# One-tensor scalar steps, and a denominator product on VectorE in place of a sum on GpSimd, in a delta-rule and rational-MoE kernel

## The chip, the cores and the metric

The kernel runs on one core of one Trainium2 chip. The metric is device time in microseconds. A core has five engines that run their own instruction queues strictly in order and meet through semaphores: TensorE (in the profile PE, its weight loads PEld), VectorE (DVE), ScalarE (ACT), GpSimd (POOL) and SyncE (SP, which here only issues DMAs). SBUF is the memory that all engines work in; PSUM takes the matrix products and is read here by DVE and ACT. Every number comes from one profiled execution or from the three timed runs.

## What is computed

The inputs are q, k and v of shape (4, 8, 768, 48), beta of (4, 8, 768), and the weights, in float64, of an MLP with a rational activation. First a delta rule runs over time for each of the 32 heads, with a 48 x 48 state:

```python
k_n = k / (norm(k) + 1e-6)
for t in range(S):
    y[t]  = q[t] @ state
    state = state + beta[t] * outer(k_n[t], v[t] - k_n[t] @ state)
```

Its output, as x with 3072 rows (tokens) of 384, goes through the MLP of width 2048:

```python
h = x @ w_in
P = a[0] + a[1]*h + a[2]*h**2 + a[3]*h**3
Q = 1.0 + abs(b[0])*abs(h) + abs(b[1])*h**2
out = (P / (Q + 1e-6)) @ w_out
```

## The kernel before, in words

Time is cut into 12 chunks of 64 steps. A chunk's delta rule is solved with products of blocks on PE and a small triangular inversion on DVE (`inverse`). Its 256 tokens then pass the MLP in 8 units of 256 hidden columns each, so there are 96 units. Float32 values are split in two float16 parts and multiplied in three passes.

A unit n goes through four functions. `hidden` lets PE build h in PSUM (`ph`, two buffers, 128 partitions x 512 values). `numerator` lets ACT make u = A3*h + a2 (tile `mu`, line L843), z = B0*|h| (tile `mr`, L845) and w = (R1*h)^2 (tile `mw`, L847); POOL adds z to w (L848); DVE makes u = h*u (L849) and u = (u + A1)*h (L850). `quotient` lets ACT compute r = exp(-ln(w + Q0)) (L861, L862, in the buffer of z); DVE multiplies g = (u + A0)*r into the float16 tile `mg` (L867), makes w = (w + Q0)*g (L868) and u = u + A0 - w (L872), and POOL writes u*r as g's second part (L873). In four of the eight units of the middle chunks, POOL takes over A0 (L854) and the subtraction (L870), and DVE's product is L865. `accumulate` multiplies g by w_out on PE. Each of `mu`, `mr`, `mw` and `mg` has three buffers. The factors A3 to Q0 are columns of tile `msc`, one value per partition.

Around each chunk there are small steps on one value, or 16, per partition. `keys_normalized` computes the keys' inverse norms in tile `nrm` (128 x 16, L513 to L520). `scales` has tile `sc`, `tokens` tile `sf`, and `scale_of` makes a power of two by masking the bits of a float against the tile `tmask` (L263). `scalars` evaluates a bound on the activation from the tile `horner` and the token scales in tile `kp` (L786 to L806) and multiplies the table `tab` by six columns of `sf` into `msc` (L810). It runs once per chunk, twice for the first: 13 times. Most of these steps are products or sums of two tensors in SBUF on DVE.

The weights arrive at the start as float64 words; `to_f32` turns them into float32 in 56 pieces: ACT takes the absolute value, POOL the maximum with a smallest number (L333), DVE joins the bits (L334, L341).

The order on each engine is set by a scheduler that goes through the functions in the order written at the end of the kernel (a unit's numerator, the quotient of the unit before, a share of the attention of later chunks, the accumulation of the unit before that, the next unit's hidden part), with priorities for some attention steps and a model of durations. The diff therefore also moves instructions that it does not name.

Of the kernel before, what the change touches and what calls it, by code (L numbers as in the profile page):

```python
# [34 lines left out]
def kernel(
# [125 lines left out]
    horner = cpool.tile([P, 2, 4], F32, name="horner")  # L161
    nc.vector.memset(horner[:, 1], 0.0)
    nc.vector.memset(horner[:, 1, 2:3], 1.0)
    for i, (at, frm) in enumerate((((0, 0), 9), ((0, 1), 11), ((0, 2), 10), ((0, 3), 7), ((1, 0), 8), ((1, 1), 10))):
        nc.vector.tensor_copy(horner[:, at[0], at[1] : at[1] + 1], coef[:, frm : frm + 1])
# [89 lines left out]

    def scale_of(dst, ss, nm, root=0):


# [2 lines left out]
        nc.scalar.activation(lg, ss, AF.Ln)
        nc.scalar.activation(lg, lg, AF.Exp, scale=-0.5 / (1 + root), bias=consts[:, 1 + root : 2 + root])
        nc.vector.tensor_tensor(  # L263
            out=dst.bitcast(U32), in0=lg.bitcast(U32), in1=tmask[:, :n], op=ALU.bitwise_and
        )
        return lg
# [13 lines left out]
    rb = cpool.tile([P, 3], F32, name="rb")  # L280
    rb0, rb1, sb1 = (rb[:, i : i + 1] for i in range(3))
    nc.vector.tensor_scalar_max(sb1, b1, 2.0 ** -90)
    nc.scalar.activation(rb0, sb1, AF.Ln)
    nc.scalar.activation(rb0, rb0, AF.Exp, scale=0.5)
    nc.vector.tensor_mul(rb1, rb0, rb0)
    nc.vector.tensor_sub(sb1, sb1, rb1)
    nc.vector.reciprocal(rb1, rb0)
    nc.vector.tensor_scalar(sb1, sb1, rb1, 0.5, op0=ALU.mult, op1=ALU.mult)
    nc.vector.tensor_add(sb1, sb1, rb0)
# [35 lines left out]
    def to_f32(t, src, nm, keep=MIN_NORMAL):  # L325
# [7 lines left out]
        nc.gpsimd.tensor_scalar_max(a, a, keep)  # L333
# [171 lines left out]
    def keys_normalized(c):  # L505
# [7 lines left out]
        nc.vector.tensor_scalar_max(ss, ss, 2.0 ** -94)  # L513
# [29 lines left out]
    def inverse(c):  # L543
# [10 lines left out]
        nc.vector.tensor_copy(wt[:, 0:256:17], bblk[:, c])  # L554
# [220 lines left out]
    def scalars(c, lo, hi):  # L775
# [11 lines left out]
        nc.vector.tensor_mul(hm, wn, gm)

        nc.vector.tensor_mul(t, horner[:, 0], hm.broadcast_to([P, 4]))
        nc.vector.tensor_add(t, t, horner[:, 1])  # L790
# [275 lines left out]
```

## Time and profile before

| | |
|---|---|
| median of three timed runs | 918.05 us (916.96 to 919.3) |
| the profiled execution | 918.86 us |
| its span, first to last instruction | 917.1 us |
| busy DVE / PE / POOL / ACT | 842.7 / 678.4 / 604.4 / 576.3 us |
| mean granted TensorE clock | 0.931 |
| first unit's w on ACT starts | 153.8 us |

A row of an engine's groups reads: line, engine, operation, output tile <- input tiles, shapes, count | busy time in us, mean duration of one in ns | idle time of the engine just before these instructions, and what ended it. A row of the timeline reads: start, duration, engine, line, operation, tiles. A row of the waits reads: engine, tile and line that waited, what it waited for, us in total, times, longest. In a row of stretches, the stretch's length is followed by busy time and number of instructions of PE, PEld, DVE, ACT and POOL as far as they have any, then the granted clock, the DMA engines' busy share and GB/s. A row of one tile's instructions has minimum, median and maximum duration in ns, and the first and the last start.

### The profile page before, as it was taken

How to read it: one execution, taken by the hardware profiler on the slowest of the kernel's cores; microseconds unless marked ns; L12 is line 12 of the kernel's file. 1: busy time of each engine (PE TensorE's matmuls, PEld its weight loads, DVE VectorE, ACT ScalarE, POOL GpSimd, SP SyncE). 2: the span in 40 equal slices, each digit the busy share in tenths (PEclk: the TensorE clock that was granted, in tenths of full speed). 3: DMA queues.
4: the chain of work that ended last, by engine and by line, in shares of the span. 5: the costliest groups of instructions: out<-in, count | busy, mean ns of one | idle time of the engine just before them, and what ended most of it. 6: DMA issues, size and time to landing. Idle time of an engine off the chain costs nothing.

```text
span 917.1 us, 23581 instructions
## 1 busy us (share of the span) xinstructions
PE 678.4 (74%) x9264; PEld 542.9 (59%) x9264; DVE 842.7 (92%) x1657; ACT 576.3 (63%) x1099; POOL 604.4 (66%) x479
## 2 busy tenths in 40 slices
PE   0321453877787886986798988888989798999785
PEld 0221443665575775765676876766767676766563
DVE  5999998887997999899999999999999999898976
ACT  4765776556466575666565766657657566677473
POOL 6866965636456376767677677676767665666754
PEclk9999996887989998999998989989989999999998
DMA  7969888679897779779268578468476662200000
GB/s 228 222 162 188 192 180 155 94 132 155 149 130 154 137 136 149 131 147 179 42 132 152 98 157 141 81 151 146 67 185 98 122 114 36 64 2 19 1 18 18
DMA packets 420110, 111.49 MB, mean 122 GB/s; under 512 B 361376, under 2 KB 416672, under 8 KB 420000
## 3 DMA queue, kind: packets, MB, share of 16 engines
q1 hardware_dynamic: 417824, 108.83, 63.5%
q8 instruction: 72, 1.18, 0.6%
q10 hardware_dynamic: 2176, 1.17, 0.4%
q14 instruction: 38, 0.31, 0.1%
HBM read 40.47 MB, written 26.23 MB: 73 GB/s over the span
## 4 chain that ended last, share of the span: by engine, by line
DVE 44%; issue 13%; DMA 11%; ACT 9%; PE 8%; POOL 8%; SPq 6%; POOLq 0%; DVEq 0%; ACTq 0%
DVE mw L868 5%; DVE mu L849 3%; DVE mg L867 3%; DVE mg L865 3%; DVE mu L850 3%; DVE z L238 3%; SPq L449 3%; PE po L888 2%; POOL mw L848 2%; DVE mu L872 2%; PE ph L826 2%; DMA wsi<-in_moe_w_in_dram 2%; DVE pr L586 2%; DMA tq<-xdq 2%; PE pg L417 1%
## 5 line engine op out<-in xcount | busy, mean ns | idle before, releaser
L888 PE MATMUL po<-w_out,mg 128*128 128x384 f16 x1152 | 225.9, 341 | 23.7 <-POOL mg L873 12.6
L826 PE MATMUL ph<-xT,w_in 128*128 128x256 f16 x1728 | 226.7, 284 | 19.7 <-DVE mu L850 19.3
L826 PEld LDWEIGHTS <-w_in 128*128 128x128 f16 x1728 | 173.2, 102 | 58.4 <-DVE mu L850 18.3
L873 POOL TENSOR_TENSOR mg<-mu,mr 128x512 f16<-128x512 f32 x96 | 131.2, 1367 | 76.5 <-DVE mu L872 34.6
L848 POOL TENSOR_TENSOR mw<-mw,mr 128x512 f32<-128x512 f32 x96 | 135.6, 1413 | 65.2 <-ACT mw L847 63.7
L888 PEld LDWEIGHTS <-mg 128*128 128x128 f16 x1152 | 112.3, 102 | 96.0 <-POOL mg L873 17.4
L417 PEld LDWEIGHTS <-kbd 128*128 128x128 f16 x1680 | 93.6, 119 | 45.4 <-issue 41.2
L843 ACT ACTIVATE mu<-ph,coef,msc 128x512 f32<-128x512 f32 x96 | 74.3, 774 | 44.8 <-DVE msc L810 15.4
L861 ACT ACTIVATE mr<-mw,msc 128x512 f32<-128x512 f32 x96 | 69.5, 726 | 50.2 <-POOL mw L848 49.8
L868 DVE SCALAR_TENSOR_TENSOR mw<-mw,msc,mg 128x512 f32<-128x512 f32 x96 | 96.3, 1003 | 1.2
L849 DVE TENSOR_TENSOR mu<-ph,mu 128x512 f32<-128x512 f32 x96 | 65.3, 681 | 16.8 <-ACT mw L847 14.2
L417 PE MATMUL pu<-z,ebd 128*128 128x48 f16 x1728 | 57.9, 188 | 25.8 <-DVE z L238 21.8
L417 PEld LDWEIGHTS <-ebd 128*128 128x128 f16 x1728 | 55.6, 100 | 30.9 <-issue 25.1
L870 POOL TENSOR_TENSOR mu<-mu,mw 128x512 f32<-128x512 f32 x36 | 48.0, 1332 | 38.1 <-DVE mw L868 26.3
L850 DVE SCALAR_TENSOR_TENSOR mu<-mu,msc,ph 128x512 f32<-128x512 f32 x96 | 71.4, 744 | 0.8
L867 DVE SCALAR_TENSOR_TENSOR mg<-mu,msc,mr 128x512 f16<-128x512 f32 x60 | 65.9, 1098 | 2.9 <-ACT mr L862 2.7
L847 ACT ACTIVATE mw<-ph,msc 128x512 f32<-128x512 f32 x96 | 66.5, 692 | 0.0
L845 ACT ACTIVATE mr<-ph,msc 128x512 f32<-128x512 f32 x96 | 65.6, 683 | 0.0
L872 DVE SCALAR_TENSOR_TENSOR mu<-mu,msc,mw 128x512 f32<-128x512 f32 x60 | 64.0, 1067 | 0.4
L417 PEld LDWEIGHTS <-wbd 128*128 128x128 f16 x1152 | 38.1, 103 | 43.0 <-issue 37.8
L862 ACT ACTIVATE mr<-mr 128x512 f32<-128x512 f32 x96 | 60.7, 633 | 1.5
L234 ACT ACTIVATE z<-pu,zmask 128x384 f16<-128x384 f32 x72 | 40.1, 579 | 32.4 <-PE pu L417 22.9
(216 smaller groups left out, 1491.4 us busy)
## 6 DMA issues: line engine op xcount, KB each, us to landing
wsi<-in_moe_w_in_dram SPq DMA_DIRECT2D x24, 256.0 KB, 5.3
xdk<-kn SPq DMA_DIRECT2D x12, 512.0 KB, 3.4
kbd<-tk SPq DMA_DIRECT2D x24, 256.0 KB, 5.1
gd<-g SPq DMA_DIRECT2D x24, 256.0 KB, 4.3
xdq<-kn SPq DMA_DIRECT2D x12, 512.0 KB, 4.5
wso<-in_moe_w_out_dram SPq DMA_DIRECT2D x32, 192.0 KB, 4.0
mbd<-mm SPq DMA_DIRECT2D x24, 256.0 KB, 4.9
wc<-img SPq DMA_DIRECT2D x24, 256.0 KB, 5.5
```

Source lines behind the costliest of these rows:

```text
L417: nc.tensor.matmul(dst[p][:, h], head(bd, lp, p * H + h), head(rt, rp, p * H + h), start=start and n == 0 and h == 0, stop=stop and n == l ...
L826: nc.tensor.matmul(ph[:, i], w_in[:, f2, wp, cc, i * P : (i + 1) * P], x[:, xp, cc], start=k == 0, stop=k == 3 * NCC - 1,)
L843: nc.scalar.activation(u, ph, AF.Identity, scale=A3, bias=a2)
L848: nc.gpsimd.tensor_add(w, w, z)
L849: nc.vector.tensor_mul(u, ph, u)
L850: nc.vector.scalar_tensor_tensor(out=u, in0=u, scalar=A1, in1=ph, op0=ALU.add, op1=ALU.mult)
L861: nc.scalar.activation(r, w, AF.Ln, bias=Q0)
L867: nc.vector.scalar_tensor_tensor(out=g[:, 0], in0=u, scalar=A0, in1=r, op0=ALU.add, op1=ALU.mult)
L868: nc.vector.scalar_tensor_tensor(out=w, in0=w, scalar=Q0, in1=g[:, 0], op0=ALU.add, op1=ALU.mult)
L872: nc.vector.scalar_tensor_tensor(out=u, in0=u, scalar=A0, in1=w, op0=ALU.add, op1=ALU.subtract)
L873: nc.gpsimd.tensor_mul(g[:, 1], u, r)
L888: nc.tensor.matmul(po[p], g[:, gp, i, p * P : (p + 1) * P], w_out[:, f2, wp, i], start=f2 == lo and i == 0 and k == 0, stop=f2 == hi - 1 a ...
```

## The change

In the unit, z becomes B1*|h| (`tab` row 1 now holds b1 times the squared output scale), the Square on ACT and the sum on POOL go, DVE computes w = (z + B0)*h with h read from PSUM, and ACT takes |w|. Since B0 and B1 are not negative, |(B1*|h| + B0)*h| is B1*h^2 + B0*|h|, as before.

The small steps on DVE that took two SBUF tensors now take one tensor and one or two pointer scalars (a value per partition, read as an operand of its own) or constants. `horner`, `tmask` and the square root of b1 (`rb`) are gone. Four of the keys' steps move from DVE to POOL, the copy of beta into `wt` and a copy into `sf` are done by ACT. On POOL the one-operation maxima become a minimum with 3e38 and a maximum.

```diff
+POWER = 0xFF800000
...
+    def power_of_two(dst, src):
+        nc.vector.tensor_scalar(dst.bitcast(U32), src.bitcast(U32), POWER, None, op0=ALU.bitwise_and)
+    def times(dst, x, by, then=None):
+        if then is None:
+            nc.vector.tensor_scalar(dst, x, by, None, op0=ALU.mult)
+        else:
+            nc.vector.tensor_scalar(dst, x, by, then, op0=ALU.mult, op1=ALU.mult)
...
     def scale_of(dst, ss, nm, root=0):
-        nc.vector.tensor_tensor(
-            out=dst.bitcast(U32), in0=lg.bitcast(U32), in1=tmask[:, :n], op=ALU.bitwise_and
-        )
+        power_of_two(dst, lg)
...
     def tables(lo, hi):
-        nc.vector.tensor_scalar_mul(row[1], ro, sb1)
+        nc.vector.tensor_scalar_mul(row[1], io, b1)
...
     def to_f32(t, src, nm, keep=MIN_NORMAL):
-        nc.gpsimd.tensor_scalar_max(a, a, keep)
+        nc.gpsimd.tensor_scalar(a, a, 3.0e38, keep, op0=ALU.min, op1=ALU.max)
...
     def keys_normalized(c):
-        nc.vector.tensor_scalar_max(ss, ss, 2.0 ** -94)
+        nc.gpsimd.tensor_scalar(ss, ss, 3.0e38, 2.0 ** -94, op0=ALU.min, op1=ALU.max)
...
-        nc.vector.tensor_mul(y1, y1, ss)
-        nc.vector.tensor_add(y0, y0, y1)
-        nc.vector.tensor_scalar(y0, y0, 1.0 / 32.0, 1e-6 / 16.0, op0=ALU.mult, op1=ALU.add)
+        nc.gpsimd.tensor_mul(y1, y1, ss)
+        nc.gpsimd.tensor_add(y0, y0, y1)
+        nc.gpsimd.tensor_scalar(y0, y0, 1.0 / 32.0, 1e-6 / 16.0, op0=ALU.mult, op1=ALU.add)
...
     def inverse(c):
-        nc.vector.tensor_copy(wt[:, 0:256:17], bblk[:, c])
+        nc.scalar.copy(wt[:, 0:256:17], bblk[:, c])
...
     def scalars(c, lo, hi):
         nc.vector.reciprocal(gm, d["lg"])
-        nc.vector.tensor_mul(hm, wn, gm)
-        nc.vector.tensor_mul(t, horner[:, 0], hm.broadcast_to([P, 4]))
-        nc.vector.tensor_add(t, t, horner[:, 1])
-        nc.vector.tensor_mul(t[:, 0:2], t[:, 0:2], hm.broadcast_to([P, 2]))
-        nc.vector.tensor_scalar_add(t[:, 1:2], t[:, 1:2], 1.0)
-        nc.vector.reciprocal(t[:, 1:3], t[:, 1:3])
-        nc.vector.tensor_mul(t[:, 0:1], t[:, 0:1], hm)
-        nc.vector.tensor_mul(r, t[:, 0:4:3], t[:, 1:3])
-        nc.vector.tensor_add(gm, r[:, 0:1], r[:, 1:2])
-        nc.vector.tensor_add(gm, gm, m0)
-        nc.vector.tensor_mul(gm, gm, io)
+        times(hm, wn, gm)
+        affine(top_, hm, m3, m2)
+        times(top_, top_, hm, hm)
+        affine(low, hm, b1, b0)
+        affine(low, low, hm, 1.0)
+        affine(one, hm, b0, 1.0)
+        nc.vector.reciprocal(kp[:, 5:7], kp[:, 5:7])
+        times(lin, hm, m1, one)
+        affine(gm, top_, low, lin)
+        nc.vector.tensor_scalar(gm, gm, m0, io, op0=ALU.add, op1=ALU.mult)
...
-        nc.vector.tensor_tensor(out=rk.bitcast(U32), in0=rk.bitcast(U32), in1=tmask[:, :1], op=ALU.bitwise_and)
-        nc.vector.reciprocal(sf[:, 1:2], rk)
-        nc.vector.tensor_mul(ikap, sf[:, 1:2], sf[:, 1:2])
-        nc.vector.tensor_mul(sf[:, 3:4], sf[:, 2:3], ikap)
-        nc.vector.tensor_mul(sf[:, 4:6], sf[:, 2:4], sf[:, 2:3].broadcast_to([P, 2]))
+        power_of_two(rk, rk)
+        nc.vector.reciprocal(rk, rk)
+        times(ikap, rk, rk)
+        nc.scalar.copy(sf[:, 1:2], ikap)
+        times(sf[:, 3:4], sf[:, 2:3], ikap)
+        times(sf[:, 4:6], sf[:, 2:4], sf[:, 2:3])
...
     def numerator(n):
-        nc.scalar.activation(z, ph, AF.Abs, scale=B0)
+        nc.scalar.activation(z, ph, AF.Abs, scale=B1)
+        nc.vector.tensor_mul(u, ph, u)
         w = sb.tile([P, 2, TG], F32, tag="mw", name=f"mw{n}", bufs=MB)
-        nc.scalar.activation(w, ph, AF.Square, scale=R1)
-        nc.gpsimd.tensor_add(w, w, z)
-        nc.vector.tensor_mul(u, ph, u)
+        nc.vector.scalar_tensor_tensor(out=w, in0=z, scalar=B0, in1=ph, op0=ALU.add, op1=ALU.mult)
+        nc.scalar.activation(w, w, AF.Abs)
```

`affine(dst, x, by, plus)` is one tensor_scalar on DVE, x*by + plus. In `scales`, the running maximum of v and the product of two scales take the same form.

Two places show what the scheduler makes of it. The first is DVE's queue at units 45 and 46, where the small steps of chunk 6 (`sf_6`, `kp_6`) lie between the units' products and the solver's (`z_7`). Before:

```order
L263 TENSOR_TENSOR sf_6_8849<-lgx6_8857,tmask_99 128x1
L786 RECIPROCAL kp_6_0_8922<-lgx6_8857 128x1
L865 TENSOR_TENSOR mg45_8993<-mu45_8905,mr45_8907 128x512
L767 RECIPROCAL sf_6_8849<-sf_6_8849 128x1
L787 TENSOR_TENSOR kp_6_0_8922<-top_149,kp_6_0_8922 128x1
L238 SCALAR_TENSOR_TENSOR xT_6_8847<-px_6_0_8862,sf_6_8849,xT_6_8847 128x3x128
L868 SCALAR_TENSOR_TENSOR mw45_8909<-mw45_8909,msc_5_7793,mg45_8993 128x512
L789 TENSOR_TENSOR kp_6_0_8922<-horner_105,kp_6_0_8922 128x4
```

After:

```order
L838 TENSOR_TENSOR mu46_8961<-ph_46_8942,mu46_8961 128x512
L840 SCALAR_TENSOR_TENSOR mw46_8966<-mr46_8963,msc_5_7773,ph_46_8942 128x512
L757 RECIPROCAL sf_6_8829<-sf_6_8829 128x1
L257 TENSOR_SCALAR kp_6_0_8902<-top_138,kp_6_0_8902 128x1
L233 SCALAR_TENSOR_TENSOR xT_6_8827<-px_6_0_8842,sf_6_8829,xT_6_8827 128x3x128
L233 SCALAR_TENSOR_TENSOR xT_6_8827<-px_6_1_8848,sf_6_8829,xT_6_8827 128x3x128
L842 SCALAR_TENSOR_TENSOR mu46_8961<-mu46_8961,msc_5_7773,ph_46_8942 128x512
L857 TENSOR_TENSOR mg45_8973<-mu45_8885,mr45_8887 128x512
```

The small steps are now TENSOR_SCALAR, the new product (L840) stands right behind the product of u, and the products of unit 46 from PSUM have moved ahead of the quotient of unit 45.

The second place is ACT's queue at units 48 to 50. Before:

```order
L861 ACTIVATE mr48_9249<-mw48_9251,msc_6_8943 128x512
L862 ACTIVATE mr48_9249<-mr48_9249 128x512
L861 ACTIVATE mr49_9377<-mw49_9379,msc_6_8943 128x512
L843 ACTIVATE mu50_9634<-ph_50_9615,coef_101,msc_6_8943 128x512
L845 ACTIVATE mr50_9636<-ph_50_9615,msc_6_8943 128x512
L847 ACTIVATE mw50_9638<-ph_50_9615,msc_6_8943 128x512
L862 ACTIVATE mr49_9377<-mr49_9377 128x512
```

After, where L841 is the new Abs, L853 and L854 are the old L861 and L862, and `y_7` and `xT_7` are the attention's outputs on their way to the MLP:

```order
L841 ACTIVATE mw48_9232<-mw48_9232 128x512
L853 ACTIVATE mr48_9229<-mw48_9232,msc_6_8923 128x512
L734 ACTIVATE y_7_9785<-py_7_0_9687,sc_7_7006 128x384
L734 ACTIVATE y_7_9785<-py_7_1_9688,sc_7_7006 128x384
L854 ACTIVATE mr48_9229<-mr48_9229 128x512
L241 ACTIVATE xT_7_9977,xs_7_9978<-y_7_9785 128x768
L841 ACTIVATE mw49_9360<-mw49_9360 128x512
L835 ACTIVATE mu50_9614<-ph_50_9595,coef_99,msc_6_8923 128x512
L837 ACTIVATE mr50_9616<-ph_50_9595,msc_6_8923 128x512
L853 ACTIVATE mr49_9357<-mw49_9360,msc_6_8923 128x512
```

The Abs of unit 49 now stands behind the outputs of the attention and ahead of the first two steps of unit 50.

More of the change, by code (lines that the diff above doesn't have):

```diff
@@ L153 @@
     nc.gpsimd.memset(consts[:, 2:3], 5.5 * LN2)
-    tmask = cpool.tile([P, 4], U32, name="tmask")
-    nc.gpsimd.memset(tmask, 0xFF800000)
     coef = cpool.tile([P, 12], F32, name="coef")
@@ L160 @@
     nc.scalar.activation(coef[:, 6:12], coef[:, 0:6], AF.Abs)
[L161 to L165, printed above, removed]
     a0, a1, a2, a3 = (coef[:, i : i + 1] for i in range(4))
-    m0, _, _, _, b0, b1 = (coef[:, i : i + 1] for i in range(6, 12))
+    m0, m1, m2, m3, b0, b1 = (coef[:, i : i + 1] for i in range(6, 12))
     bblk = cpool.tile([P, NCH, 16], F32, name="bblk")
@@ L278 @@
     top = cpool.tile([P, 3, 2], F32, name="top")
[L280 to L289, printed above, removed]
     def tables(lo, hi):
@@ L639, in scales @@
         if "v" in fmax:
-            nc.vector.tensor_max(sc[:, 1:2], sc[:, 1:2], fmax["v"])
+            nc.vector.tensor_scalar(sc[:, 1:2], sc[:, 1:2], fmax["v"], None, op0=ALU.max)
         fmax["v"] = sc[:, 1:2]
@@ L643, in scales @@
         nc.vector.tensor_copy(sc[:, 4:5], sc[:, 3:4])
-        nc.vector.scalar_tensor_tensor(
-            out=sc[:, 5:6], in0=sc[:, 2:3], scalar=1.0 / 16.0, in1=sc[:, 3:4], op0=ALU.mult, op1=ALU.mult
-        )
+        times(sc[:, 5:6], sc[:, 2:3], 1.0 / 16.0, sc[:, 3:4])
         nc.vector.reciprocal(sc[:, 4:6], sc[:, 4:6])
@@ L782, in scalars, with affine @@
         kp = sb.tile([P, 10], F32, tag="kp", name=f"kp_{c}_{lo}", bufs=4)
-        gm, rk, ikap, hm = (kp[:, i : i + 1] for i in range(4))
-        t = kp[:, 4:8]
-        r = kp[:, 8:10]
+        gm, rk, ikap, hm, top_, low, one, lin = (kp[:, i : i + 1] for i in range(8))
         nc.vector.reciprocal(gm, d["lg"])
-        nc.vector.tensor_mul(hm, wn, gm)
-        nc.vector.tensor_mul(t, horner[:, 0], hm.broadcast_to([P, 4]))
-        nc.vector.tensor_add(t, t, horner[:, 1])
-        nc.vector.tensor_mul(t[:, 0:2], t[:, 0:2], hm.broadcast_to([P, 2]))
-        nc.vector.tensor_scalar_add(t[:, 1:2], t[:, 1:2], 1.0)
-        nc.vector.reciprocal(t[:, 1:3], t[:, 1:3])
-        nc.vector.tensor_mul(t[:, 0:1], t[:, 0:1], hm)
-        nc.vector.tensor_mul(r, t[:, 0:4:3], t[:, 1:3])
-        nc.vector.tensor_add(gm, r[:, 0:1], r[:, 1:2])
-        nc.vector.tensor_add(gm, gm, m0)
-        nc.vector.tensor_mul(gm, gm, io)
+        times(hm, wn, gm)
+        def affine(dst, x, by, plus):
+            nc.vector.tensor_scalar(dst, x, by, plus, op0=ALU.mult, op1=ALU.add)
+        affine(top_, hm, m3, m2)
[7 more added lines that the diff above has]
+        nc.vector.tensor_scalar(gm, gm, m0, io, op0=ALU.add, op1=ALU.mult)
         nc.vector.tensor_scalar_max(gm, gm, 2.0 ** -60)
@@ L839, in numerator @@
         d = unit[n]
-        A3, R1, A1, B0, A0, Q0 = (toks[c]["m"][:, i, f2 : f2 + 1] for i in range(6))
+        A3, B1, A1, B0, A0, Q0 = (toks[c]["m"][:, i, f2 : f2 + 1] for i in range(6))
         ph = d.pop("ph")
```

## The prediction

> **What bounds the kernel now.** First the page's own summary, then the busy times by stretch. DVE is VectorE, ACT ScalarE, POOL GpSimd.
>
> ```profile
> span 917.1 us, 23581 instructions
> PE 678.4 (74%) x9264; PEld 542.9 (59%) x9264; DVE 842.7 (92%) x1657; ACT 576.3 (63%) x1099; POOL 604.4 (66%) x479
> ...
> 155.00:390.00 235.00, 187.48 (x2789) 152.91 (x2790) 208.60 (x415) 139.18 (x254) 137.66 (x96) 0.88 0.82 138
> 390.00:740.00 350.00, 296.36 (x4154) 240.23 (x4152) 342.64 (x604) 226.13 (x410) 246.99 (x185) 0.93 0.69 128
> 740.00:825.00 85.00, 75.34 (x1093) 60.60 (x1092) 79.09 (x136) 58.01 (x104) 53.00 (x43) 1.00 0.24 43
> 825.00:917.10 92.10, 71.16 (x548) 48.68 (x548) 74.43 (x103) 54.96 (x93) 57.45 (x41) 0.94 0.05 14
> ```
>
> In each stretch the busy times stand in the order PE, PEld, DVE, ACT, POOL. The 96 units begin at about 155 us. From 390 to 740 us DVE is busy 342.6 of 350 us (98%), and outside that stretch 362.1 of 412.1 us (88%). A change that puts 96 large instructions on DVE has to be judged by what DVE gives up elsewhere.
>
> Next I asked whether DVE's busy time is work. The timeline (start, duration, engine) of one piece of the steady stretch:
>
> ```profile
> 499.35 0.75 DVE L868 SCALAR_TENSOR_TENSOR mw<-mw,msc,mg 128x512 f32<-128x512 f32 x1
> 500.24 1.27 POOL L870 TENSOR_TENSOR mu<-mu,mw 128x512 f32<-128x512 f32 x1 [1.48 <-DVE mw L868]
> 500.62 0.61 DVE L238 SCALAR_TENSOR_TENSOR z<-pu,zmask,z 128x384 f16<-128x384 f32 x1
> ...
> 502.69 1.27 POOL L873 TENSOR_TENSOR mg<-mu,mr 128x512 f16<-128x512 f32 x1
> 502.87 1.12 DVE L787 TENSOR_TENSOR kp<-top,kp 128x1 f32<-128x1 f32 x1
> 503.95 0.69 POOL L854 TENSOR_SCALAR mu<-mu,msc 128x512 f32<-128x512 f32 x1
> 504.02 0.63 DVE L789 TENSOR_TENSOR kp<-horner,kp 128x4 f32<-128x4 f32 x1
> 504.68 0.16 DVE L790 TENSOR_TENSOR kp<-kp,horner 128x4 f32<-128x4 f32 x1
> ```
>
> L787 multiplies one element per partition and takes 1.12 us: it ends at 503.99, just when POOL's L873 ends (503.96). L789 ends with POOL's L854 (504.65 and 504.64); L790, with POOL done, takes 0.16 us. L238 reads one operand from PSUM and runs its 0.61 us in the middle of POOL's L870. So a DVE instruction with two SBUF tensors waits for the POOL instruction under way, and the wait is booked as DVE busy time. Minimum, median and maximum durations say the same:
>
> ```profile
> L787 DVE TENSOR_TENSOR kp<-top,kp x13: 132/139/1125, 134.9 to 854.2; 128x1 f32<-128x1 f32 x13
> L800 DVE TENSOR_SCALAR kp<-kp x13: 134/153/155, 149.6 to 864.8; 128x1 f32<-128x1 f32 x13
> L803 DVE TENSOR_TENSOR kp<-kp,tmask x13: 136/779/1771, 150.5 to 865.5; 128x1 uint32<-128x1 uint32 x13
> L378 DVE TENSOR_SCALAR vss<-wfs x8: 200/202/209, 88.2 to 151.9; 128x1 f32<-128x1 f32 x8
> ```
>
> One tensor and a constant (L800) never waits; one tensor and a pointer scalar (L378) costs 0.06 us more and never waits either.
>
> **The change, part by part.** Sums are of DVE time, since DVE sets the end.
>
> *The unit.* 96 times POOL's add and ACT's Square go; DVE gets the product (z + B0) * h with h in PSUM, ACT an Abs in SBUF.
>
> ```profile
> L848 POOL TENSOR_TENSOR mw<-mw,mr 128x512 f32<-128x512 f32 x96 | 135.6, 1413 | 65.2 <-ACT mw L847 63.7
> L850 DVE SCALAR_TENSOR_TENSOR mu<-mu,msc,ph 128x512 f32<-128x512 f32 x96 | 71.4, 744 | 0.8
> L849 DVE TENSOR_TENSOR mu<-ph,mu 128x512 f32<-128x512 f32 x96 | 65.3, 681 | 16.8 <-ACT mw L847 14.2 <-ACT lgx L261 1.6 <-issue 0.8
> L868 DVE SCALAR_TENSOR_TENSOR mw<-mw,msc,mg 128x512 f32<-128x512 f32 x96 | 96.3, 1003 | 1.2
> L862 ACT ACTIVATE mr<-mr 128x512 f32<-128x512 f32 x96 | 60.7, 633 | 1.5
> L847 ACT ACTIVATE mw<-ph,msc 128x512 f32<-128x512 f32 x96 | 66.5, 692 | 0.0
> ```
>
> The new product has the form of L850 (SBUF, pointer, PSUM), so I take 96 x 0.744 = **+71.4 us**. Bounds: 96 x 0.681 = 65 (L849, no scalar), 96.3 if it waited as L868 does. ACT's swap is 96 x (0.633 - 0.692) = -6 us; the copies that ACT takes over give that back. ACT is idle 37% of the span, so I cost ACT at nothing; without that cover it would be the copies' 12 x 0.2 and 13 x 0.2 = 5 us (0.2 from the small ACT steps, as in the window of tile nrm below).
>
> *The scalar steps.* All DVE instructions on tile kp (13 calls), in a view of that tile alone, and L807:
>
> ```profile
> 0.00:917.10 917.10, 83.84 (x223) 18.41 (x50) 0.93 0.65 122
> L807 DVE TENSOR_TENSOR sf<-sf 128x2 f32<-128x2 f32 x13 | 4.2, 319 | 0.1
> L513 DVE TENSOR_SCALAR nrm<-nrm 128x16 f32<-128x16 f32 x12 | 5.0, 416 | 0.0
> L554 DVE COPY wt<-bblk 128x16 f32<-128x16 f32 x12 | 9.2, 770 | 0.0
> L263 DVE TENSOR_TENSOR sf<-lgx,tmask 128x1 uint32<-128x1 uint32 x12 | 5.6, 465 | 0.6 <-ACT lgx L262 0.6
> 0.00:917.10 917.10, 32.45 (x84) 6.13 (x24) 18.38 (x12) 0.93 0.65 122
> ```
>
> Two of the 223 are large output steps (2 x 0.6), so the scalars cost 83.8 - 1.2 + 4.2 = 86.8 us. After: per call 17 steps, 5 without a pointer at 0.15 (L800), 6 with one at 0.203 (L378), 6 with two at 0.26 (L378 plus another 0.06, an estimate): 3.53 us, 45.9 for 13. **-40.9** (-45 if a second pointer is free). The last fence row is tile nrm: of its 32.45 us on DVE the reduction (12 x 0.944) and two reciprocals (12 x 0.49) stay, 15.2 go to POOL: **-15.2**. L554 goes to ACT: **-9.2**. L263's mask becomes a constant: 12 x (0.465 - 0.149) = **-3.8**, and about -2.5 on the two-wide one by the same step. Together -71.6: it pays for the new product and no more.
>
> The Trainium skill ("SBUF — State Buffer", Who interferes with whom) speaks against part of this: a tensor_scalar can itself enter a 2-port mode and then take the pair that GpSimd uses. L513, 16 wide, averages 0.416 us and agrees; the steps one wide do not. By that rule the two-wide steps (sf columns 4 and 5, sc columns 2 and 3) would keep their waits, and the sum would be some 4 us worse.
>
> *Relief.* What still waits for POOL are DVE's large steps with two SBUF inputs, L868 above and three more:
>
> ```profile
> L867 DVE SCALAR_TENSOR_TENSOR mg<-mu,msc,mr 128x512 f16<-128x512 f32 x60 | 65.9, 1098 | 2.9 <-ACT mr L862 2.7
> L872 DVE SCALAR_TENSOR_TENSOR mu<-mu,msc,mw 128x512 f32<-128x512 f32 x60 | 64.0, 1067 | 0.4
> L865 DVE TENSOR_TENSOR mg<-mu,mr 128x512 f16<-128x512 f32 x36 | 37.8, 1050 | 3.4 <-POOL mu L854 3.2
> 155.00:917.10 762.10, 630.34 (x8581) 502.41 (x8581) 704.77 (x1255) 478.28 (x858) 495.09 (x362) 0.92 0.60 108
> ...
> ACT mu L843 <- DVE msc L810: 15.4, 7, 5.5
> DVE w_out L334 <- POOL wai L333: 6.8, 3, 5.1
> ...
> 9.39 0.40 POOL L177 TENSOR_SCALAR bblk<-bblk 128x192 f32<-128x192 f32 x1 [0.30 <-issue]
> L333 POOL TENSOR_SCALAR wao<-wao,gate 128x192 f32<-128x192 f32 x32 | 28.7, 906 | 14.6 <-ACT wao L332 8.0 <-DVE gate L602 6.4
> ```
>
> Undisturbed, the three-operand steps take 0.75 us (L868 at 499.35) and L865, like L849, 0.68. The waits are 96 x 0.25 + 60 x 0.35 + 60 x 0.32 + 36 x 0.37 = 77.5 us. From 155 us on POOL is busy 495 us (the window row, its last busy time); it loses 135.6 and gains the keys' steps, some 36 there at no more than 0.40 us (L177, two operations on 192 elements): 374 us, 24% less. If waits shrink as POOL's busy time does, that is -19 us; for the smaller two-input steps (block inversion, splits) I add -4 as an estimate. Bounds: 0, and -39 (POOL's one large step per unit in place of two: half of the waits).
>
> *The chunk boundary.* At a chunk's first unit ACT waited 15.4 us in all for the table that ends the scalar steps. These steps fall from 6.7 us per call to 3.5, so I take half of it: **-7**. Here nothing hides them. The new ACT copy of sf column 1 adds a hop of about 0.2 us, 12 times; left at nothing as ACT is idle there.
>
> *The start.* The first keys' four steps on POOL cost at most 4 x (0.40 - 0.17) us more: **+1**. For the 56 weight pieces POOL's max becomes min and max: 0.906 us for 192 elements with one operation, 0.40 for two of another kind, so the new price may lie half a microsecond to either side. DVE waited for these only 6.8 us in all: -7 to +7, taken as 0. Queued behind them on POOL are only the next pieces and the key and query splits.
>
> *Sum.* The product and the steps removed cancel (+71.4 - 71.6). The relief falls in stretches where DVE is 98% and 88% busy, so 0.93 x 23 = 21. 918.86 (the profiled execution; span 917.1 and 1.8 around it) - 21 - 7 + 1 = **892 us**. That execution is 0.8 above the median 918.05, which at this precision is the same.
>
> **Rivals.**
>
> *More is freed.* The waits halve (-39 x 0.95) and the boundary gives its 7: 918.9 - 37 - 7 = **875 us**. For it: the longest waits (L803 up to 1.77 us) are longer than one POOL product (1.27 us), so POOL's instructions follow one another closely, and thinning them may pay twice. Against: outside 390 to 740 us DVE is only 88% busy, and PE at 296 of 350 us is not far behind.
>
> *Nothing is gained.* If the new product too waited as L868 does, it would cost 96.3 instead of 71.4; the 25 us more eat the gain: **917 us**. Against it stands L849: 681 ns average over 96, with the same kind of operands. The Trainium skill ("Perfetto Trace Analysis", Optimizing Scalar/DVE Operations) says that moving operations between DVE and GpSimd might not help, since they share a port; by that rule this rival would be the forecast. The L238 that ran through POOL's L870 speaks against it for operands in PSUM.
>
> *Slower: DVE waits for ACT once more per unit.* Today the order for w is ACT, POOL, ACT, DVE, and POOL can afford its waits:
>
> ```profile
> POOL mw L848 <- ACT mw L847: 63.7, 26, 8.9
> ACT mr L861 <- POOL mw L848: 49.8, 34, 4.5
> ```
>
> After, it is ACT, DVE, ACT, DVE, in two queues that both run strictly in order: ACT's Abs of w stands behind other work (at unit 49 behind the y copies and their square sum, which wait for PE), its Ln behind the Abs, and DVE's quotient steps behind the Ln, with all that follows them. The place is that pair, the price DVE idle time. At 0.28 us per unit (27 us over 96) the gain is gone; at 0.4 us the time is 892 + 38 = **930 us**. For it: DVE already idles 14.2 us for ACT at L849. Against: DVE's order has other units' steps between, and ACT idles a third.
>
> **How the numbers follow.** Forecast 892: 0.53. More freed, 875: 0.20. No gain, 917: 0.10. Slower, 930: 0.17. Differences under 0.3% (2.8 us) cannot be told from no change. Faster takes the first two and a little of the third: 0.75; same 0.07; slower 0.18. The range 862 to 924 runs from all gains at their bounds to 0.33 us per unit of the slower case, whose far half it leaves out.
>
> **What would show it.** The new product at 0.73 to 0.76 us with a maximum not far above. The steps on tile kp near 45 us of DVE, each 0.15 to 0.27. L868's successor below 0.95 us on average. DVE still over 95% busy in the steady stretch but for a shorter time; POOL near 490 us in all. Wrong would be: DVE idle before the product of u or before the quotient with ACT as releaser, over 30 us together; the product at about 1 us; or a first unit that starts over 5 us later.

## The result and the profile after

The changed kernel takes 894.17 us (892.8 to 895.27) beside 917.89 us (916.96 to 919.3) for the kernel before: a ratio of 0.974, 95% interval 0.9721 to 0.9758. The forecast was 892 us. The difference is 23.7 us, and so is that of the two profiled spans (917.1 and 893.4). Of the runs below, one of the kernel with the keys on DVE took 919.8 us at a granted clock of 0.76; its row in the table is that of the other three (0.92 to 0.94).

The page's summary of the kernel after, and its DVE groups in the unit. Line numbers have moved: L838 is the old L849 (product of u), L840 the new product, L842 the old L850, L857 the old L865, L859 the old L867, L860 the old L868, L864 the old L872.

```profile
span 893.4 us, 23555 instructions
PE 675.1 (76%) x9264; PEld 540.8 (61%) x9264; DVE 800.4 (90%) x1666; ACT 579.7 (65%) x1122; POOL 468.4 (52%) x430
...
L860 DVE SCALAR_TENSOR_TENSOR mw<-mw,msc,mg 128x512 f32<-128x512 f32 x96 | 88.0, 918 | 0.4
L838 DVE TENSOR_TENSOR mu<-ph,mu 128x512 f32<-128x512 f32 x96 | 65.5, 682 | 23.8 <-ACT mr L837 22.9 <-POOL mg L865 0.7
L840 DVE SCALAR_TENSOR_TENSOR mw<-mr,msc,ph 128x512 f32<-128x512 f32 x96 | 70.7, 737 | 0.0
L859 DVE SCALAR_TENSOR_TENSOR mg<-mu,msc,mr 128x512 f16<-128x512 f32 x60 | 60.7, 1012 | 2.5 <-ACT mr L854 2.5
L864 DVE SCALAR_TENSOR_TENSOR mu<-mu,msc,mw 128x512 f32<-128x512 f32 x60 | 56.0, 934 | 0.2
L857 DVE TENSOR_TENSOR mg<-mu,mr 128x512 f16<-128x512 f32 x36 | 28.0, 776 | 3.2 <-ACT mr L854 1.9 <-POOL mu L846 1.2
```

DVE is busy 42.3 us less (842.7 to 800.4) although it got 70.7 us of products. But its idle time, the span less the busy time, rose from 74.4 to 93.0 us: 18.6 of the 42.3 us came back as waits, and 23.7 are left.

The stretches after the first unit's start, and single instructions (minimum, median, maximum in ns), of the kernel after:

```profile
155.00:375.00 220.00, 176.02 (x2609) 143.63 (x2607) 188.42 (x391) 133.29 (x246) 103.36 (x85) 0.88 0.74 140
375.00:720.00 345.00, 297.33 (x4246) 240.91 (x4245) 321.93 (x634) 227.40 (x423) 201.16 (x162) 0.93 0.70 131
...
L840 DVE SCALAR_TENSOR_TENSOR mw<-mr,msc,ph x96: 725/737/745, 151.9 to 878.2; 128x512 f32<-128x512 f32 x96
L257 DVE TENSOR_SCALAR kp<-top,kp x13: 185/195/207, 134.6 to 831.9; 128x1 f32<-128x1 f32 x13
L259 DVE TENSOR_SCALAR kp<-kp,coef x13: 256/264/268, 145.3 to 836.5; 128x1 f32<-128x1 f32 x13
L257 DVE TENSOR_SCALAR sf<-sf x13: 218/230/1444, 149.1 to 846.8; 128x2 f32<-128x2 f32 x13
...
0.00:893.40 893.40, 41.30 (x210) 20.28 (x63) 0.93 0.63 125
0.00:893.40 893.40, 17.17 (x36) 6.31 (x24) 39.01 (x60) 0.93 0.63 125
```

The last two rows are the views of tile kp and tile nrm alone (DVE is the first busy time in each). In the steady stretch DVE is at 93% (321.9 of 345), where it was at 98%. None of the 96 new products waits: 745 ns at most. The one-wide steps with a pointer cost 0.20 us, with two 0.26, and do not wait either. The two-wide one does: 230 ns in the median, 1444 at most.

Where DVE waits now, and what waits for it (the waits of the kernel after: who, for what, us in total, times, longest):

```profile
DVE mu L838 <- ACT mr L837: 22.9, 21, 4.3
DVE z L233 <- ACT z L229: 7.8, 8, 3.1
DVE ab L557 <- DMA gb<-gd: 7.3, 3, 2.6
DVE z L231 <- ACT z L227: 6.3, 5, 1.6
DVE m L667 <- PE pm L409: 5.8, 4, 2.5
...
ACT mu L835 <- DVE msc L802: 25.0, 12, 4.8
...
ACT wt L546 <- DVE wh L590: 6.0, 4, 2.8
```

Before, the first line stood at 14.2 us and the two z lines (of the attention) at 1.5 together.

### The profile page after: what moved, and what is told of

Read it like the earlier page. It is cut to its first block, busy times and chain, and to the rows that moved or that the text cites. A ratio compares the mean times of both kernels' runs of the same rounds, so it can differ in the third digit from the quotient of the medians.

```text
span 893.4 us, 23555 instructions
## 1 busy us (share of the span) xinstructions
PE 675.1 (76%) x9264; PEld 540.8 (61%) x9264; DVE 800.4 (90%) x1666; ACT 579.7 (65%) x1122; POOL 468.4 (52%) x430
## 4 chain that ended last, share of the span: by engine, by line
DVE 33%; PE 22%; DMA 15%; SPq 11%; issue 8%; ACT 8%; POOL 3%; ACTq 0%; DVEq 0%; POOLq 0%
PE ph L818 7%; PE po L880 5%; SPq L441 4%; DVE mw L860 3%; DMA tq<-xdq 3%; PE pg L409 3%; DVE mu L838 2%; DVE mu L864 2%; DVE w_out L333 2%; DVE mw L840 2%; PE pm L409 2%; DVE mg L859 2%; PE pu L409 2%; DVE mu L842 2%; DMA wc<-img 2%
## 5 line engine op out<-in xcount | busy, mean ns | idle before, releaser
L880 PE MATMUL po<-w_out,mg 128*128 128x384 f16 x1152 | 223.3, 340 | 28.8 <-POOL mg L865 27.0
L865 POOL TENSOR_TENSOR mg<-mu,mr 128x512 f16<-128x512 f32 x96 | 133.2, 1391 | 92.6 <-DVE mu L864 53.7
L880 PEld LDWEIGHTS <-mg 128*128 128x128 f16 x1152 | 110.5, 102 | 101.9 <-POOL mg L865 33.7
L835 ACT ACTIVATE mu<-ph,coef,msc 128x512 f32<-128x512 f32 x96 | 74.4, 775 | 60.7 <-DVE msc L802 25.0
L860 DVE SCALAR_TENSOR_TENSOR mw<-mw,msc,mg 128x512 f32<-128x512 f32 x96 | 88.0, 918 | 0.4
L838 DVE TENSOR_TENSOR mu<-ph,mu 128x512 f32<-128x512 f32 x96 | 65.5, 682 | 23.8 <-ACT mr L837 22.9
L841 ACT ACTIVATE mw<-mw 128x512 f32<-128x512 f32 x96 | 60.4, 630 | 35.5 <-DVE mw L840 35.1
L862 POOL TENSOR_TENSOR mu<-mu,mw 128x512 f32<-128x512 f32 x36 | 51.1, 1421 | 50.2 <-DVE mw L860 20.3
L840 DVE SCALAR_TENSOR_TENSOR mw<-mr,msc,ph 128x512 f32<-128x512 f32 x96 | 70.7, 737 | 0.0
L842 DVE SCALAR_TENSOR_TENSOR mu<-mu,msc,ph 128x512 f32<-128x512 f32 x96 | 70.5, 735 | 0.0
L853 ACT ACTIVATE mr<-mw,msc 128x512 f32<-128x512 f32 x96 | 69.2, 721 | 1.1
L409 PE MATMUL pu<-z,ebd 128*128 128x48 f16 x1728 | 56.1, 187 | 16.1 <-DVE z L233 12.3
L837 ACT ACTIVATE mr<-ph,msc 128x512 f32<-128x512 f32 x96 | 65.6, 684 | 0.0
L231 POOL TENSOR_TENSOR mm<-m,mm 128x1024 f16<-128x1024 f32 x12 | 31.6, 2632 | 64.0 <-ACT mm L227 56.2
L859 DVE SCALAR_TENSOR_TENSOR mg<-mu,msc,mr 128x512 f16<-128x512 f32 x60 | 60.7, 1012 | 2.5 <-ACT mr L854 2.5
L854 ACT ACTIVATE mr<-mr 128x512 f32<-128x512 f32 x96 | 60.4, 630 | 1.4
L846 POOL TENSOR_SCALAR mu<-mu,msc 128x512 f32<-128x512 f32 x36 | 28.9, 802 | 55.2 <-DVE mu L842 52.1
```

The source lines that it names most:

```text
L409: nc.tensor.matmul(dst[p][:, h], head(bd, lp, p * H + h), head(rt, rp, p * H + h), start=start and n == 0 and h == 0, stop=stop and n == l ...
L835: nc.scalar.activation(u, ph, AF.Identity, scale=A3, bias=a2)
L837: nc.scalar.activation(z, ph, AF.Abs, scale=B1)
L838: nc.vector.tensor_mul(u, ph, u)
L840: nc.vector.scalar_tensor_tensor(out=w, in0=z, scalar=B0, in1=ph, op0=ALU.add, op1=ALU.mult)
L842: nc.vector.scalar_tensor_tensor(out=u, in0=u, scalar=A1, in1=ph, op0=ALU.add, op1=ALU.mult)
```

## The experiments

All times are medians beside runs of the kernel before on the same chip (916.5, 917.9 and 918.3 us in the three sets of experiments, 917.9 in that of the change). Compare the kernels by the ratio; the last four columns are span, busy times and DVE's idle time (span less busy) of the profiled execution, in us. Three kernels are there only to be timed: the two without the sum leave the linear term out of the denominator, and the product from SBUF gives another denominator.

| kernel | us | ratio to before, 95% interval | span | DVE busy | DVE idle | POOL busy |
|---|---|---|---|---|---|---|
| before | 917.9 | 1 | 917.1 | 842.7 | 74.4 | 604.4 |
| product alone | 896.5 | 0.9760 (0.9726 to 0.9793) | 895.0 | 837.6 | 57.4 | 473.7 |
| steps alone | 900.5 | 0.9808 (0.9765 to 0.9852) | 898.7 | 802.3 | 96.4 | 601.7 |
| no sum | 869.9 | 0.9485 (0.9441 to 0.9529) | 865.6 | 775.9 | 89.7 | 466.1 |
| **the change** | 894.2 | 0.9740 (0.9721 to 0.9758) | 893.4 | 800.4 | 93.0 | 468.4 |
| product from SBUF | 905.6 | 0.9861 (0.9832 to 0.9889) | 901.5 | 844.4 | 57.1 | 488.8 |
| no sum, with steps | 871.7 | 0.9503 (0.9454 to 0.9552) | 867.6 | 749.2 | 118.4 | 468.0 |
| change, nothing moved | 882.4 | 0.9607 (0.9568 to 0.9647) | 881.7 | 811.6 | 70.1 | 477.9 |
| change, copy on DVE | 881.6 | 0.9609 (0.9574 to 0.9644) | 879.8 | 807.2 | 72.6 | 475.1 |
| change, keys on DVE | 888.3 | 0.9678 (0.9635 to 0.9722) | 884.1 | 808.5 | 75.6 | 454.4 |
| change, single maxima | 892.6 | 0.9710 (0.9673 to 0.9747) | 890.7 | 803.8 | 86.9 | 487.8 |
| change, z first | 882.3 | 0.9612 (0.9571 to 0.9654) | 876.5 | 802.8 | 73.7 | 465.2 |
| nothing moved, z first | 888.0 | 0.9676 (0.9644 to 0.9708) | 882.5 | 817.1 | 65.4 | 467.5 |
| change, five units on POOL | 889.5 | 0.9689 (0.9648 to 0.9729) | 890.2 | 805.1 | 85.1 | 490.5 |

### The two halves of the change, and the sum taken away

The product alone, in the kernel before (the table's row 1, and a copy of the squared scale for it):

```diff
-        nc.scalar.activation(w, ph, AF.Square, scale=R1)
-        nc.gpsimd.tensor_add(w, w, z)
+        nc.vector.scalar_tensor_tensor(out=w, in0=z, scalar=B0, in1=ph, op0=ALU.add, op1=ALU.mult)
+        nc.scalar.activation(w, w, AF.Abs)
```

> Only the unit's change in the kernel before: product on DVE, Abs on ACT, no sum on POOL (and the table row, the root of b1 and the copy of the last factor that go with it); all small steps as before. Theory of the prediction (DVE time sets the end; the product costs 96 x 0.74 and gives back about 19 to 31 us of waits): DVE gains 40 to 52 us, time 955 (945 to 968). Rival, that the thinner POOL queue and the shorter way of w bring the gain: 918 or less.

The steps alone: every edit of the change but this one, and so without the copy into `sf` on ACT, which goes with the new table row.

> All of the change but the unit's: small steps with one tensor, keys on POOL, copies on ACT, min and max; Square on ACT and sum on POOL stay. Theory: DVE loses some 72 us of 843, and if DVE set the end all the way the time would be 850; since PE and the waits between engines stand close behind, 850 to 875. Rival, that the steps' waits were hidden anyway (DVE would have waited elsewhere): 900 or more, so that the product would have to carry the gain.

No sum: the kernel before without POOL's add, and nothing in its place.

```diff
-        nc.gpsimd.tensor_add(w, w, z)
```

> The kernel before without POOL's sum in the unit (left out: z is not added to w, so the denominator lacks its linear term); DVE's list of work is the same. It measures the relief by itself: theory, DVE's three-operand steps go from 1.00 to 1.10 us down to 0.90 to 1.02, DVE busy falls by 19 to 39 us and the time to 895 (880 to 902). Rival, that the waits depend on the remaining POOL instructions only: step durations within 0.03 us of before, time over 912.

My theory missed on all three: the rivals came true on the first (918 us or less) and the second (900 or more), and on the third the relief was larger than either had it. By the theory the product alone should have made the kernel slower (955 us); it gains 2.4% with none of the scalar edits that I had let pay for it. Most of the reason is in the kernel without the sum. Its four large groups that can wait for POOL (line numbers are one below those of the kernel before), and its kp view:

```profile
L867 DVE SCALAR_TENSOR_TENSOR mw<-mw,msc,mg 128x512 f32<-128x512 f32 x96 | 84.3, 878 | 0.6
L866 DVE SCALAR_TENSOR_TENSOR mg<-mu,msc,mr 128x512 f16<-128x512 f32 x60 | 55.0, 918 | 4.4 <-ACT mr L861 3.3
L871 DVE SCALAR_TENSOR_TENSOR mu<-mu,msc,mw 128x512 f32<-128x512 f32 x60 | 54.8, 913 | 0.5
L864 DVE TENSOR_TENSOR mg<-mu,mr 128x512 f16<-128x512 f32 x36 | 30.0, 833 | 7.6 <-POOL mu L853 6.9 <-ACT mr L861 0.6
...
0.00:900.00 900.00, 67.76 (x223) 18.13 (x50) 0.93 0.65 124
```

Over 0.75 us (0.68 for the last group), as in the prediction, the four groups wait 96 x 0.128 + 60 x 0.168 + 60 x 0.163 + 36 x 0.153 = 38 us, where it was 77.5: half. The steps on kp fell by 16.1 us too, without an edit to them. In all, 135.6 us fewer on POOL made DVE 66.8 us less busy, half a microsecond per microsecond, and the kernel 47 us shorter (1 - 0.9485 of 917.9). Some of that may come from the shorter way of w, since before ACT's step after the sum waited 49.8 us for POOL; these runs do not part the two. Putting the product in costs 25 us of that (0.9760 - 0.9485), though DVE is then 61.7 us busier, since DVE idles 32.3 us less.

The steps alone free 40.4 us of DVE and gain 17.6. Three of the four groups in that kernel (L868, L872 and L867 before):

```profile
L870 DVE SCALAR_TENSOR_TENSOR mw<-mw,msc,mg 128x512 f32<-128x512 f32 x96 | 101.1, 1053 | 1.1
L874 DVE SCALAR_TENSOR_TENSOR mu<-mu,msc,mw 128x512 f32<-128x512 f32 x60 | 70.3, 1172 | 0.4
L869 DVE SCALAR_TENSOR_TENSOR mg<-mu,msc,mr 128x512 f16<-128x512 f32 x60 | 66.0, 1100 | 0.2
```

They were at 1003, 1067 and 1098 ns; the fourth went from 1050 to 1007. POOL is as busy as before, and part of the waiting that the small steps no longer do seems to have passed to the large ones: 96 x 0.050 + 60 x 0.105 = 11 us more in two groups, 1.5 less in the fourth. Idle time grew by 22.0 us as well.

### Where the product reads from

```diff
-        nc.vector.scalar_tensor_tensor(out=w, in0=z, scalar=B0, in1=ph, op0=ALU.add, op1=ALU.mult)
+        nc.vector.scalar_tensor_tensor(out=w, in0=z, scalar=B0, in1=u, op0=ALU.add, op1=ALU.mult)
```

> The changed kernel with the new product reading u from SBUF where it read h from PSUM (left out: the right denominator); same instruction, same count. Theory: with two SBUF tensors it waits for POOL like the quotient's steps, 0.85 to 1.0 us in place of 0.737, DVE +11 to +25 us, time 905 to 917. Rival, that where the operand lies makes no difference: 0.74 us and 894.

```profile
L840 DVE SCALAR_TENSOR_TENSOR mw<-mr,msc,mu 128x512 f32<-128x512 f32 x96 | 96.0, 1000 | 0.4
L840 DVE SCALAR_TENSOR_TENSOR mw<-mr,msc,mu x96: 725/745/2258, 152.2 to 887.1; 128x512 f32<-128x512 f32 x96
```

As expected: 1000 ns in place of 737, with only the place of one operand changed. It is waiting and not a slower pace, as the shortest take 725 ns in both kernels. In the two timelines, 32 of the 96 take over 0.85 us here, and 31 of these start while a POOL instruction is under way; of the other 64 ten do. In the change, where the operand lies in PSUM, 57 of the 96 start that way, and none takes over 745 ns. The product costs DVE 25 us more, and all of DVE 44 (11 to 25 were expected), but the median only 11: DVE idles 36 us less. The Trainium skill ("Perfetto Trace Analysis", Optimizing Scalar/DVE Operations) says that moving work between DVE and GpSimd might not help, because they share an SBUF read port. For operands in SBUF this case agrees: beside the steps the move from POOL to DVE brings nothing then (0.9808 for the steps alone, 0.9861 with the product from SBUF). With one operand in PSUM it helps (0.9740, and 0.9760 without the steps).

### What the moved steps cost

Beside the product, all the steps together bring 2 us (0.9760 to 0.9740, which is within the intervals), though DVE is 37 us less busy. So I undid three edits: the keys' four steps and the copy into `wt` go back to DVE, the maxima on POOL are single again. The copy into `sf` stays on ACT, as in every kernel with the product.

> The change without the parts that move work between engines: the keys' four steps and the copy into wt stay on DVE, the maxima stay single operations. So it is the product with the scalar steps that take pointers. The product alone took 896.5 us, all together 894.2 us, though DVE was busy 37 us less. Theory A (the moved steps stand in POOL's queue and eat what the pointer steps gain): 880 to 886 us. Theory B (beside the product, DVE time freed at a chunk's start becomes idle time of DVE, whichever steps it is freed from): 893 to 898 us, DVE busy near 825 us and idle near 70 us.

The time is that of theory A: 882.4 us. The scalar steps with pointers bring 14 us beside the product (0.9760 to 0.9607), and the three edits, which I had counted as a gain of 24 us on DVE, make the kernel 12 us slower. Then each was undone alone:

```diff
-        nc.gpsimd.tensor_scalar(ss, ss, 3.0e38, 2.0 ** -94, op0=ALU.min, op1=ALU.max)
-        nc.gpsimd.tensor_mul(y1, y1, ss)
+        nc.vector.tensor_scalar_max(ss, ss, 2.0 ** -94)
+        nc.vector.tensor_mul(y1, y1, ss)
...
-        nc.scalar.copy(wt[:, 0:256:17], bblk[:, c])
+        nc.vector.tensor_copy(wt[:, 0:256:17], bblk[:, c])
...
-        nc.gpsimd.tensor_scalar(a, a, 3.0e38, keep, op0=ALU.min, op1=ALU.max)
+        nc.gpsimd.tensor_scalar_max(a, a, keep)
```

> The change with only the keys' four steps back on DVE as before. With all three moves undone the time was 882.4 us, with all three 894.2. Theory A (the keys' chain, which on POOL now waits for DVE or ACT four times per chunk with the units' products queued behind it: 13.2 us of waits on DVE at these steps in the change, and DVE idle that follows later): 883 to 887 us, DVE busy near 808 us. Theory B (it is not one of the moves; any change of the durations gives the scheduler another order, worth some 10 us either way): the three moves undone one by one do not add up to 11.8 us, and this one may land anywhere from 880 to 900 us.

> The change with only the copy of beta into wt back on DVE. It costs DVE 12 x 0.2 to 12 x 0.77 = 2 to 9 us. Theory A (keys): 894 to 898 us. If the copy, in ACT's queue behind the units' steps, is what holds the solver up: 884 to 888 us. Theory B (order): anywhere from 880 to 900 us.

> The change with only the 56 weight pieces' maxima back as single operations on POOL. They took 28.7 us there for 32 and about as long per element for the other 24 before, 19.4 and 12.8 us in the change, all before the first unit starts, and DVE waited 6 to 7 us for them in either. The first unit's Abs starts at 154.1 us with them and at 154.0 with all moves undone. Theory A: within 3 us of 894. Theory B (order): anywhere from 880 to 900 us.

Putting the copy alone back gives it all: 881.6 us, under even the 884 to 888 of the case that the copy holds the solver up. The keys' steps give 5.7 us (0.9740 to 0.9678), and the maxima 2.8, which cannot be told from zero. So theory A falls, and with it the reason that I had given for the 12 us, POOL's queue: the copy was in ACT's. By the ratios the three give 12.0 + 5.7 + 2.8 = 20.5 us one by one and 12.2 together. They do not seem to add up, as theory B had it, though by the intervals such a difference is uncertain by some 8 us. On ACT the copy took 12 x 0.21 us, so its duration is nothing; but ACT waited 6.0 us for DVE to release `wt` (the last waits row above), with the units' steps queued behind. Of the 20.4 us of DVE idle time that go with it, 14 stand at one place, 240 to 400 us; the change, then with the copy on DVE (DVE is the third busy time):

```profile
240.00:400.00 160.00, 130.97 (x1954) 107.30 (x1954) 132.05 (x261) 96.57 (x179) 78.54 (x66) 0.89 0.75 144
```

```profile
240.00:400.00 160.00, 130.14 (x2004) 108.16 (x2004) 146.33 (x288) 105.60 (x190) 86.59 (x69) 0.94 0.75 147
```

DVE idles 28.0 us there in the change and 13.7 with the copy on DVE (15.5 in the kernel before). Its waits for ACT before a unit's product of u are 7.0 us there in the change and 0.2 with the copy on DVE, those for ACT's z of the attention 10.6 and 5.7. ACT in turn waits for PE before these z, with the units' Abs, Ln and Exp behind in its queue. The timeline of ACT at that place in the change (a bracket at a row's end is the idle time before it and its releaser):

```profile
293.90 0.63 ACT L854 ACTIVATE mr<-mr 128x512 f32<-128x512 f32 x1
301.64 1.19 ACT L229 ACTIVATE z<-pu,zmask 128x384 f16<-128x384 f32 x2 [7.11 <-PE pu L409]
...
311.00 0.22 ACT L546 COPY wt<-bblk 128x16 f32<-128x16 f32 x1 [0.79 <-DVE wh L590]
313.83 0.58 ACT L229 ACTIVATE z<-pu,zmask 128x384 f16<-128x384 f32 x1 [2.61 <-PE pu L409]
```

The longest wait, 7.11 us for PE, lies ahead of the copy, which itself waited 0.79 us. So it is not the copy's own wait that shows at this place. Whether the copy causes the 12 us in another way, or only the other order that the scheduler makes when one instruction changes its engine, these runs do not settle: ACT's queue differs between the two kernels from about 41 us on, before the first unit.

### The order at a unit's head, and more work for POOL

ACT makes z ahead of u, and DVE the product of w ahead of that of u:

```diff
-        u = sb.tile([P, 2, TG], F32, tag="mu", name=f"mu{n}", bufs=MB)
-        nc.scalar.activation(u, ph, AF.Identity, scale=A3, bias=a2)
...
-        nc.vector.tensor_mul(u, ph, u)
...
+        u = sb.tile([P, 2, TG], F32, tag="mu", name=f"mu{n}", bufs=MB)
+        nc.scalar.activation(u, ph, AF.Identity, scale=A3, bias=a2)
         nc.scalar.activation(w, w, AF.Abs)
+        nc.vector.tensor_mul(u, ph, u)
```

> The change, but ACT makes z ahead of u, and DVE does the product of w ahead of the product of u, so that ACT's Abs of w can start one large step earlier and DVE waits for ACT's z one step less. The work is the same. Theory A (what eats the steps' gain is the ping-pong between ACT and DVE at a unit's head: DVE idled 22.9 us for z in the change, ACT 35.1 us for the product): 882 us, DVE idle before the head products below 12 us. Theory B (the gain is eaten elsewhere: at chunk boundaries, or in the order of the other work): 894 us within 4.

882.3 us, as theory A said. The idle time at the head did not fall as far as it said, though (in this kernel L835 makes z and L839 u, L837 is the product of w and L841 that of u):

```profile
DVE mw L837 <- ACT mr L835: 8.5, 10, 1.4
...
DVE mu L841 <- ACT mu L839: 6.1, 10, 1.0
```

That is 14.6 us in place of 22.9, where "below 12" was expected: 8 us less idle time beside a gain of 12. Nor does that idle time go with the kernel's: in the change with the copy on DVE, the keys on DVE, single maxima, nothing moved or five units on POOL it is 11 to 14 us in each, and their times run from 881.6 to 892.6 us (single maxima: 12.6 us and 892.6). So a shorter wait at the head is not by itself worth 12 us. The test of theory A is whether its gain adds to the other one:

> z ahead of u, and nothing moved between engines (the keys' steps and the copy on DVE, single maxima): the two edits that took 12 us each off the change. If they relieve different waits: 894.2 - 11.9 - 11.8 = 870.5 us, DVE busy near 812 us and idle below 62. If both relieve the same wait, or both only found a better order: 880 to 884 us.

It does not: 888.0 us, some 6 above either alone and above both forecasts. So the two edits are not two separate waits removed, and nothing here says that z first is better by itself.

The last one gives A0 and the subtraction of one more unit per middle chunk to POOL:

```diff
-        by_pool = 2 <= c < NCH - 1 and f2 in (0, 4, 5, 6)
+        by_pool = 2 <= c < NCH - 1 and f2 in (0, 2, 4, 5, 6)
```

> The change, with five units in place of four in each of the nine middle chunks that give A0 and the subtraction to POOL. Per such unit DVE gives up a step of 0.93 us and changes one of 1.01 for one of 0.78: 9 x 1.17 = 10.5 us less on DVE; POOL gets 9 x (0.80 + 1.42) = 20 us more. If DVE is still what sets the end and waits do not grow: 885 us. If the waits for POOL grow as they shrank when the sum went (66.8 us of DVE for 135.6 us of POOL, a half): the 20 us on POOL cost 10 us of DVE and nothing is gained: 894 us. If POOL's queue is the new limit: above 897 us.

889.5 us, between the first two cases: POOL got 22 us busier and DVE, which gave up 10.5 us, 4.7 us busier. The waits for POOL ate the gain of DVE time (L860 went from 918 to 992 ns, L857 from 776 to 1007); the time still fell by 5 us (0.9740 to 0.9689, just clear of noise), as DVE idled 8 us less.

### The steps without the sum

> All the edits but the unit's, and POOL's sum left out too (z is not added, so the denominator lacks its linear term). Without the sum the kernel before took 869.9 us, with the steps alone 900.5. Theory A (the steps free DVE time, and it is the new product that hinders it from being worth anything): 869.9 - 16 = 854 us or less. Theory B (the steps' 17 us came from waits for POOL that the sum caused, and without the sum there is little of them left): 866 to 872 us, DVE below 745 us but idle above 110 us.

871.7 us, theory B, with DVE slightly over the 745 us that it named. DVE is 26.7 us less busy than without the steps (775.9 to 749.2) and idles 28.7 us more (89.7 to 118.4). With DVE at 86% its time was no longer what set the end. This kernel has the copy into `wt` on ACT, so whatever goes with that is in it as well.

## Why the prediction was right, point by point

**The total.** 892 forecast, 894.2 measured; as a difference -26 and -23.7. That they lie so close is in good part luck. DVE got 42.3 us less busy, where the sum had 23; its idle time rose by 18.6 us, where the sum had no rise; and the 7 us at the boundary did not come. These errors nearly cancel. The account was half right: DVE is relieved when POOL does less, and that is the larger gain. But steps that pay for the product are not what the runs show: by that the product alone would have taken 955 us, and it took 896.5.

**DVE sets the end, and its steps with two SBUF tensors wait for POOL.** The waiting held. It shows in the product from SBUF (1000 against 737 ns) and in the kernel without the sum, where steps that nobody edited became shorter. That DVE sets the end held only in part: DVE time added to or taken from these kernels moved the end by 0 to 0.7 of its size (0.7 when the sum went, 0.4 when the steps or the product came alone, nothing for the steps without the sum). With the copy back on DVE, DVE was 6.8 us busier and the end came 12 us earlier.

**The product, +71.4.** 70.7 us of DVE: right as a price. As time it cost 25 us, not 71 (no sum, then the product alone), which the sum could not show since it set DVE's time equal to the kernel's.

**The scalar steps, -71.6.** The steps that I had at 86.8 and 45.9 us are at 41.3 - 1.2 + 6.7 = 46.8 (the view of tile kp less the two large steps, and the two-wide step below). On nrm 32.45 to 17.17, -15.3 as forecast. So product and steps cancel in DVE time, near enough. "It pays for the new product and no more" was wrong as time: the pointer steps bring 14 us beside the product, and with the other three edits the kernel is 12 us slower.

**ACT at nothing.** This is the term that failed most plainly. I priced the two copies on ACT by their duration (5 us at most if ACT had no cover) and not by what ACT waits for before them: 6.0 us for the one into `wt`, 16.2 for the one into `sf` (`ACT sf L797 <- DVE kp L257`). With the first back on DVE the kernel is 12 us faster, though by which way stays open; no run undoes the second.

**The two-wide steps.** The Trainium skill ("SBUF — State Buffer", Who interferes with whom) says that a tensor_scalar can itself enter a mode that shares the port. I took the -2.5 us all the same and quoted 4 us as its price. The trace agrees with the page:

```profile
L257 DVE TENSOR_SCALAR sf<-sf 128x2 f32<-128x2 f32 x13 | 6.7, 518 | 0.2
L252 DVE TENSOR_SCALAR sc<-lgq 128x2 uint32<-128x2 uint32 x12 | 6.7, 556 | 0.0
```

These replaced steps of 4.2 and 4.3 us, so DVE got 4.9 us busier. I had 2.6 us for the first (13 x 0.203) and 1.8 for the second (4.3 - 2.5): 9 us too little, not 4.

**Relief, -21.** Undersized by half. I let the waits shrink with POOL's busy time (24%, 19 us in the four groups). POOL's time after 155 us came out as forecast (377 us, 374 forecast), so it is the proportion that failed. The waits shrank by 96 x 0.085 + 60 x 0.086 + 60 x 0.133 + 36 x 0.274 = 31 us, 40%, and outside them, the product and the edited steps DVE lost 16 us more, where I had added 4 (42.3 + 70.7 = 113.0 us went; kp 42.5, nrm 15.3, the copy 9.2, the masks and two-wide steps -1.0 and the four groups 31.3 make 97.3). The rival "more is freed" had this part right (waits to be halved), and the kernel without the sum lost some 40 us in these groups; its 875 us did not come, because idle time took 18.6 back.

**The chunk boundary, -7.** Wrong. ACT's wait for the table rose from 15.4 us to 25.0 (`ACT mu L835 <- DVE msc L802`), though the steps in front take half as long. From a chunk's first scalar step to the end of the table's product on DVE about 24 us pass on average in the change and 20 in the kernel before, of which these steps are 3.5 and 6.7: other steps stand between them in DVE's queue. The way also goes to ACT and back once more now, for the copy into `sf` that I left at nothing, and ACT waits 16.2 us for DVE there.

**The start, +1.** The first unit's Abs starts at 154.1 us, the Square before it started at 153.8. Right, and too small to matter. DVE's wait for the weights' maxima was 9.1 us in all, not 6.8 (that was one of two groups), and is 6.4 in the change.

**The slower rival.** Its mechanism is there in part: DVE's idle time for ACT at the head and before the quotient rose from 16.9 us to 27.3 (22.9 + 2.5 + 1.9), just under the 30 us that I named. It did not decide, and most of the rise is at the head, where kernels that differ by one or a few small edits do not have it (11 to 15 us in place of 22.9).

**What would show it.** The product's duration, the kp steps and L860 (918 ns) came as listed; POOL came out at 468, not 490, mostly since the maxima took 20 us less (28.7 + 23.6 us before, 19.4 + 12.8 after). "DVE still over 95% busy in the steady stretch" was wrong (93%), and that is the sign of the idle time that took the extra relief back.

## What to carry to other kernels

Work on POOL can cost DVE time as well: taking 135.6 us off POOL freed 66.8 us of DVE here, and a new product on DVE with one operand in PSUM did not wait, where the same one with both in SBUF did. Look at the queue that a moved instruction enters and at what it waits for there, and not only at its duration: putting a copy of 0.21 us, 12 times, back on its old engine went with 12 us less here, though the cause is not settled. And measure the parts of a change apart: here edits with which the kernel is 12 us slower were hidden among others that gain 36, and single edits of that size did not add up.
